# Sliding-window attention into a SwiGLU FFN on one core: constants from a broadcast word, loads ahead of GpSimd's masks, and a new order table

## The chip, the cores and the metric

One core of one Trainium2 chip runs the whole program. The metric is the device time of one execution in microseconds (us). A core has five engines that run their own instruction streams in order: TensorE (PE, matrix products; its weight loads are shown as PEld), VectorE (DVE), ScalarE (ACT), GpSimd (POOL) and SyncE (SP, which here only issues transfers). Streams wait for one another by semaphores. Transfers are issued by an engine and run on 16 DMA engines, which all queues share.

## The reference

Inputs are q, k, v of shape 4 x 8 x 768 x 64 (batch, heads, sequence, head size) and the FFN's weights. Attention is masked to a window of 128 keys and to 4 "sink" keys at the sequence's start; its output becomes x with 3072 tokens x 512.

```python
keep = (pos[None, :] < 4) | ((rel >= 0) & (rel < 128))      # rel = query - key
a = softmax(where(keep, q @ k.T / sqrt(64), -1e9))
x = (a @ v).transpose(0, 2, 1, 3).reshape(3072, 512)
xn = x / sqrt(mean(x * x) + 1e-6) * rms_g
g = xn @ w_gate                                             # 512 x 1536
out = (g * sigmoid(g) * (xn @ w_val)) @ w_out               # 1536 x 512, float32 out
```

## The kernel before

**Blocks and groups.** The 3072 tokens are 24 blocks of 128 (six per batch entry); four blocks make a group of 512 tokens for the FFN, six groups in all. Matrix products take bf16. Lines are those of the kernel before; behind the part that the diff cuts away, a line has a number lower by two in the kernel after.

**Loads.** q and k of block 0 come as float32 through SP's hardware queue and are cast on chip (`load_f32`, L345; the cast, L349). All other blocks of q, k (L353) and v (L357) and all weights (w_gate and w_val L399, w_out in two halves L405) are loads that GpSimd issues on the software queue, casting to bf16 on the way. That queue takes them in order. In the text a load has the name of its tensor and block (q.9, k.6, v.5), or of the weight and its first 128-column part (wg.8). A load of a block from the tenth on needs the scores of ten blocks before, since its buffers are reused. The n-th load also waits until the eighth load before it has landed.

**Transposes.** Scores need q and k with the head dimension on the partitions. Blocks 0 to 7 are transposed on TensorE (`pe_t`, L445) and copied out by DVE or ACT (L452). From block 8 on, SP issues a DMA transpose (`dma_t`, L459). The same split holds for the normalised tokens that feed the FFN: TensorE (L708, copied at L714) for blocks 0 to 7, a DMA transpose by SP (`dma_x`, L720) from block 8 on. SP also issues the stores of the output (L1020). All of SP's transfers stand in one in-order stream: one that waits for its input holds all behind it.

**Attention of a block.** Scores on TensorE (L485, L501, and L563 for blocks cut into triangles), exponentials on ACT (L512, L536, L572), the mask on DVE (L520, L547, L584) for blocks below 16 and on GpSimd as `affine_select` (L526, L597) from block 16 on, then the product with v (L616, L621, and the sink keys' part, L641). In the first two blocks the mask is added by TensorE instead, as a product of the identity with a bias tile (L467). DVE divides (L660, L661), ACT squares (L669), and DVE makes the RMS factor and scales (L676 to L693).

**FFN of a group.** Gate and value products (L975), tanh on ACT (L982), two DVE operations (L988, L998), the output product (`project`, L1008), evacuation on ACT (L1016), the store (L1020). A group's parts are 128 tokens x 4 columns of 128 in group 0, 256 tokens x 2 in groups 1 and 2, and 512 tokens x 1 from group 3 on.

**Constants.** An identity tile and a bias tile are made at the start: DVE sets each to zero (L275, L276), GpSimd's `affine_select` then writes the diagonal (L286) and the triangle (L292). DVE derives the identity without the sink rows (L304), the second bias half (L298) and the masks from them. 56 "warm" products of a zero tile (L421) on TensorE have no effect on the result; they keep that engine running.

**The order.** Every operation is recorded in a `Plan` with what it needs and what it gives. Nothing is scheduled at run time: `ORDER` has, for each engine, the list of operation numbers in the order in which that engine runs them, `TURNS` interleaves the five lists into the order in which the instructions are written out, and `BANKS` names the PSUM bank for each product. `Plan.run` plays the three tables and asserts that each operation's needs have been given before:

```python
        for c in "".join(turns.split()):
            e, ops = ids[c]
            o = self.ops[next(ops)]
            assert o["needs"] <= given, o["gives"]
```

In the kernel before, GpSimd issues the loads up to q.20, then runs the masks of block 16 and of a part of block 17, issues k.20, runs another mask, and so on to v.23. SP's transposes begin q.8, q.9, k.8, k.9, q.10, then the store of block 0, q.11, k.10, k.11.

Of the kernel before, what the change touches and what calls it, by code (L numbers as in the profile page):

```python
# [9 lines left out]
ALU = mybir.AluOpType  # L10
ACT = mybir.ActivationFunctionType
FP32 = mybir.dt.float32
BF16 = mybir.dt.bfloat16
I32 = mybir.dt.int32

P = 128
# [7 lines left out]
NEG = -32768.0  # L24
# [10 lines left out]
class Plan:  # L35
# [5 lines left out]
    def __init__(self):  # L41
        self.ops, self.held = [], {}

    def op(self, ways, needs=(), gives=(), prio=0.0, takes=(), drops=(), ring=None, work=0.0,
           mode=0):
        self.ops.append(dict(
            ways=ways, needs=set(needs), gives=tuple(gives), prio=prio, takes=tuple(takes),
            drops=tuple(drops), ring=ring, work=work, mode=mode, at=len(self.ops),
        ))
# [40 lines left out]
""",  # L90
    "ACT": """
24 20 22 199 177 175 178 176 182 180 181 183 168 188 222 204-206 211 207 212 209 191 210
217 226 228 227 229 195 598 220 236 603 613 618 608 243 633 628 260 623 245 247 246 248
638 278 262 255 264-267 197 280 282 284 653 273 320 648 643 295 297 659 290 322 299 301
300 302 276 324 325 293 326 327 309 664 678 669 683 674 333 312 693 340 316 341 688 342
343 698 355-357 336 358 703 370 371 708 372 318 373 349 385 364 387 718 713 723 739 379
399 401 400 402 728 418 419 733 420 393 421 409 763 758 778 768 754 773 744 749 427 433
414 783 434-436 448 449 793 450 798 451 442 808 788 819 803 463-466 813 457 824 480 475
482 494 496 497 495 513 488 514 515 504 834 838 516 848 843 853 829 863 868 858 878 873
525 883 531-533 893 509 888 534 899 923 549-551 928 552 938 543 567-569 918 570 585 587  # L100
933 943 948 561 953 579 958 909 904 968 593 963 914 973 1008 1003 994 998 1013 1028 1023
989 1038 1018 1033 984 1053 1048 1043 979 1069 1059 1064 1072 1073
""",
    "DVE": """
# [13 lines left out]
""",  # L118
    "POOL": """
25 8 9 26-28 31 34 30 32 37 35 29 38 33 39 41 42 40 43 45 47 44 48 46 49 36 50 53 57 52  # L120
54 51 56 63 62 60 55 58 64 61 59 65-99 467 469 468 470 481 100 483 101-108 517 520 109
518 519 535 538 537 536 110 553 555 554 571 573 556 572 588 586 574
""",
    "SP": """
# [7 lines left out]
ASDDSDGDPDPSPDPPPPPGPPPGPDPGPPDDPGAGPPPPADGPPPPGPPSPDPSADPGSDPSPGAAAPAGPAPPDAPPGPPAPDPAP  # L132
PPPADPGPDAGPPDPPDGAPPGPAPPAGDPAPAPDGADAPDGPAPPPADPAGPDAPADAGPPPPAPADGAPADGPPPPPAPPDPGPPD
DPAGPDPAGPDPGAPDDGPDGPDADGDPDGPADADPGAADPGPGDPADGAPDPGADAPGADADPGDPAPPDAPPDADAPGDPPADAGP
AAGPAPDAPPDPADPDAPGDAPDDGDPAPGDPPGSAAPGADAPGDPDGPPPDAGDAPGDADPPGADPAGDSAPPAGASPADPADSADP
PPGADAPGPSADDPGASAPGDPGSAPPGDPSADGAPDASDAPPDADPAGPPSAAADPAADPADPDAPAGADPGADPPDAPPADDPDGS
PDAPASAGDPPAPAGDSPADAPADDPPAGSADPPDASDPAGPADPSDDPGAPDDPADAPDGSDPDGPAGAPADSAPPADSDPPDGPDS
PDAGASPAAPDASGDPADSPDSDPGSPPPDDPSDGPDADPAPADPSDPSPDPSPDDAPDPDAPADPADAPDADAPDPDPASAPDASAP
DSADPADPDPASAPASADPAPPDASDPDAPSDASPADPDADPDPDPDAPASAPPDASADPAGPDGPGDPDGAPDPDPDPDAPAAGPSA
# [16 lines left out]
def kernel(  # L156
# [128 lines left out]
    def make_ident():  # L285
        nc.gpsimd.affine_select(  # L286
            out=ident, in_=ident, compare_op=ALU.not_equal, fill=1.0,
            base=0, pattern=[[-1, P]], channel_multiplier=1,
        )
# [851 lines left out]
```

## Time and profile before

| | us |
|---|---|
| median of 3 runs (lowest, highest) | 241.71 (241.26, 241.87) |
| the profiled execution, its own time | 243.59 |
| its span | 241.9 |
| TensorE busy in it | 231.3 (96%) |
| DVE busy | 187.4 (77%) |
| ACT busy | 122.8 (51%) |
| GpSimd busy | 89.2 (37%) |
| granted TensorE clock, mean | 1.000 of full speed |

The profile is one execution, recorded by the hardware. Its page has the busy time of each engine (part 1), the span in 40 equal slices of about 6 us with the busy share in tenths (part 2), the DMA queues (part 3), the chain of work that ended last (part 4), and the costliest groups of instructions (part 5). Further views are the waits (engine, line, what it waited for: total, times, longest), the chain as a list in order of time, a timeline, and a table of stretches: for each stretch its length, then the busy time of PE, PEld, DVE, ACT and POOL (with the number of instructions), the granted clock, the mean DMA share and GB/s. In a stretch an instruction counts where it starts. A DMA's time is from its issue to its landing.

### The profile page before, as it was taken

What the parts mean: (1) busy time and instruction counts of PE and PEld (TensorE: products, weight loads), DVE (VectorE), ACT (ScalarE), POOL (GpSimd) and SP (SyncE); (2) the same over time, 40 slices, a digit from 0 to 9 for tenths busy, and PEclk for the clock granted to TensorE, in tenths of its full rate; (3) what the DMA queues carried; (4) which work ended last, traced back from release to release, by engine and by line L of the source; (5) the groups of instructions that cost most, each with busy time, mean ns of one, the idle gap of its engine ahead of it and who ended that gap; (6) DMA issues with size and microseconds to landing.
All of it is one profiled execution on the core that took longest, in us unless ns stands there. A gap on an engine that the chain in (4) does not pass through costs nothing.

```text
span 241.9 us, 5897 instructions
## 1 busy us (share of the span) xinstructions
PE 231.3 (96%) x2329; PEld 147.6 (61%) x2354; DVE 187.4 (77%) x478; ACT 122.8 (51%) x267; POOL 89.2 (37%) x116
## 2 busy tenths in 40 slices
PE   7889999999879999999999999999999999999995
PEld 5568986876668776777876644445554444444443
DVE  3599989989979999999898989994569946537520
ACT  4776368667766574337654464454543321233112
POOL 8985894597526554000004982022540000000000
PEclk9999999999999999999999999999999999999999
DMA  9999999999999999999601999527010114101024
GB/s 128 143 183 195 182 178 194 162 143 139 137 151 152 138 143 154 132 233 156 126 2 24 119 150 123 131 70 128 3 23 0 32 36 173 43 0 47 0 87 173
DMA packets 113741, 27.42 MB, mean 113 GB/s; under 512 B 103857, under 2 KB 110769, under 8 KB 113714
## 3 DMA queue, kind: packets, MB, share of 16 engines
q0 software_dynamic: 81760, 13.90, 79.3%
q1 hardware_dynamic: 31810, 12.95, 29.8%
q8 instruction: 18, 0.29, 0.5%
q10 hardware_dynamic: 144, 0.20, 0.2%
q14 instruction: 9, 0.07, 0.1%
HBM read 28.35 MB, written 6.29 MB: 143 GB/s over the span
## 4 chain that ended last, share of the span: by engine, by line
PE 67%; DMA 20%; POOL 6%; issue 2%; DVE 2%; SPq 2%; POOLq 0%
PE v L975 20%; PE o L1008 20%; PE g L975 18%; DMA wo<-in_moe_w_out_dram 5%; DMA qkT<-q 4%; DMA wv<-in_moe_w_val_dram 4%; DMA wg<-in_moe_w_gate_dram 3%; DMA q<-in_q_dram 3%; POOL v L357 2%; SPq L459 2%; PE s L563 2%; PE av L621 2%; POOL k L353 1%; PE av L616 1%; PE o_last L1028 1%
## 5 line engine op out<-in xcount | busy, mean ns | idle before, releaser
L975 PE MATMUL v<-xnt,wv 128*128 128x128 bf16 (+2 forms) x527 | 72.2, 282 | 0.4 <-DMA wv<-in_moe_w_val_dram 0.2
L975 PE MATMUL g<-xnt,wg 128*128 128x128 bf16 (+2 forms) x521 | 71.3, 281 | 0.4
L1008 PE MATMUL o<-wo,hT 128*128 128x512 bf16 x259 | 65.3, 379 | 1.1 <-issue 0.5
L982 ACT ACTIVATE th<-g 128x512 bf16<-128x512 f32 x72 | 41.7, 599 | 48.4 <-PE g L975 48.2
L988 DVE SCALAR_TENSOR_TENSOR p<-th,g 128x512 bf16<-128x512 bf16 x72 | 48.1, 682 | 18.9 <-ACT th L982 18.7
L975 PEld LDWEIGHTS <-wv 128*128 128x128 bf16 x528 | 43.3, 98 | 21.3 <-DMA wv<-in_moe_w_val_dram 0.6
L998 DVE TENSOR_TENSOR hT<-p,v 128x512 bf16<-128x512 bf16 x72 | 48.1, 682 | 9.3 <-PE v L975 7.8
L975 PEld LDWEIGHTS <-wg 128*128 128x128 bf16 x528 | 42.8, 98 | 19.3 <-issue 1.0
L1008 PEld LDWEIGHTS <-hT 128*128 128x128 bf16 x276 | 25.4, 98 | 26.5 <-issue 0.2
L597 POOL TENSOR_SCALAR_AFFINE_SELECT e<-e 128x512 bf16<-128x512 bf16 x20 | 12.7, 656 | 54.4 <-ACT e L572 53.0
L572 ACT ACTIVATE e<-s 128x384 bf16<-128x384 f32 x52 | 23.1, 495 | 12.5 <-PE s L563 12.5
L1016 ACT ACTIVATE osb<-o 128x512 f32<-128x512 f32 x23 | 13.4, 597 | 21.8 <-PE o L1008 18.0
L357 POOL DMA_DIRECT2D v<-in_v_dram x24 | 21.3, 888 | 8.5 <-DMA q<-in_q_dram 3.8
L353 POOL DMA_DIRECT2D q<-in_q_dram x23 | 20.4, 891 | 9.9 <-DMA k<-in_k_dram 6.7
L353 POOL DMA_DIRECT2D k<-in_k_dram x23 | 20.4, 889 | 9.1 <-DMA v<-in_v_dram 4.5
L669 ACT ACTIVATE sq<-x 128x512 bf16<-128x512 bf16 x24 | 15.1, 631 | 14.8 <-DVE x L661 14.5
L661 DVE TENSOR_TENSOR x<-av,rden 128x256 bf16<-128x256 f32 x48 | 20.4, 424 | 1.7
L693 DVE SCALAR_TENSOR_TENSOR xr<-x,r,gb 128x512 bf16<-128x512 bf16 x24 | 18.7, 778 | 0.8
L621 PE MATMUL av<-v,e 128*128 128x65 bf16 x192 | 16.4, 193 | 0.3 <-DMA v<-in_v_dram 0.3
L536 ACT ACTIVATE e<-s 128x512 bf16<-128x512 f32 (+1 forms) x36 | 15.1, 519 | 1.6 <-PE s L485 1.5
L616 PE MATMUL av<-v,e 128*128 128x65 bf16 x160 | 14.8, 193 | 0.0
L621 PEld LDWEIGHTS <-e 128*128 128x128 bf16 x192 | 12.7, 97 | 2.8 <-DVE e L547 0.4
(78 smaller groups left out, 192.6 us busy)
## 6 DMA issues: line engine op xcount, KB each, us to landing
out_dram<-osb SPq DMA_DIRECT2D x23, 256.0 KB, 2.2
v<-in_v_dram POOLq DMA_DIRECT2D x24, 128.0 KB, 8.9
q<-in_q_dram POOLq DMA_DIRECT2D x23, 128.0 KB, 8.1
k<-in_k_dram POOLq DMA_DIRECT2D x23, 128.0 KB, 9.6
wo<-in_moe_w_out_dram POOLq DMA_DIRECT2D x2, 768.0 KB, 11.3
wg<-in_moe_w_gate_dram POOLq DMA_DIRECT2D x5, 256.0 KB, 8.0
wv<-in_moe_w_val_dram POOLq DMA_DIRECT2D x5, 256.0 KB, 8.9
stage<-in_k_dram SPq DMA_DIRECT2D x1, 256.0 KB, 3.0
```

The source lines that it names most:

```text
L353: nc.gpsimd.dma_start(out=T[name, g], in_=block_of(src, g))
L357: nc.gpsimd.dma_start(out=V16[b][:, t, :, 0:D], in_=block_of(v, g))
L572: nc.scalar.activation(out=e_tile(g)[:, x:x + 2, 0:TW], in_=BANK.pop(("s", g, u, hi))[:, 0:2 * TW].rearrange("p (j c) -> p j c", c=TW), fu ...
L616: nc.tensor.matmul(out=dest, lhsT=T["e", g - 1][:, x, P:2 * P], rhs=V16[b][:, t - 1, h, :], start=(t == 1), stop=False, skip_group_check=True,
L621: nc.tensor.matmul(out=dest, lhsT=T["e", g][:, x, 0:P], rhs=V16[b][:, t, h, :], start=(t == 0), stop=True, skip_group_check=True,)
L661: nc.vector.tensor_tensor(out=T["x16", g][:, 4 * u:4 * u + 4, :], in0=pvv[:, :, 0:D], in1=rden.unsqueeze(2).to_broadcast((P, 4, D)), op=AL ...
L693: nc.vector.scalar_tensor_tensor(out=T["xr", g], in0=T.pop(("x16", g)).rearrange("p h d -> p (h d)"), scalar=r[:, 3:4], in1=gb, op0=ALU.mu ...
L975: nc.tensor.matmul(out=ps[:, i * n:(i + 1) * n], lhsT=w_sb[:, kt, ft * P:(ft + 1) * P], rhs=T["xnt", G][:, kt, cols], start=(kt == 0), sto ...
L982: nc.scalar.activation(out=T["th", key], in_=BANK[("g", key)], func=ACT.Tanh, scale=0.5,)
L988: nc.vector.scalar_tensor_tensor(out=T["p1", key], in0=T.pop(("th", key)), scalar=1.0, in1=BANK.pop(("g", key)), op0=ALU.add, op1=ALU.mult,)
L998: nc.vector.tensor_tensor(out=T[hk][:, i:i + n, cols], in0=T.pop(("p1", key)).rearrange("p (n c) -> p n c", n=n), in1=BANK.pop(("v", key)) ...
L1008: nc.tensor.matmul(out=BANK[("o", G, tb)], lhsT=T["h", G, ft // 4][:, ft % 4, tb * P:(tb + 1) * P], rhs=wo[:, ft, :], start=(ft == 0), sto ...
```

## The change

Two memsets by DVE go, and with them two operations of the plan, so all numbers shift by two (1077 operations become 1075). The two `affine_select`s read a constant of the program, a float32 zero broadcast over 128 x 128, in place of the tile that they write; they need nothing any more. `Plan` gets a table of aliases that is empty. `ORDER`, `TURNS` and `BANKS` are new; `...` marks what is cut.

```diff
-        self.ops, self.held = [], {}
+        self.ops, self.held, self.alias = [], {}, {}
...
-            ways=ways, needs=set(needs), gives=tuple(gives), prio=prio, takes=tuple(takes),
+            ways=ways, needs={x for t in needs for x in self.alias.get(t, (t,))}, gives=tuple(gives), prio=prio, takes=tuple(takes),
...
     "POOL": """
-25 8 9 26-28 31 34 30 32 37 35 29 38 33 39 41 42 40 43 45 47 44 48 46 49 36 50 53 57 52
-54 51 56 63 62 60 55 58 64 61 59 65-99 467 469 468 470 481 100 483 101-108 517 520 109
-518 519 535 538 537 536 110 553 555 554 571 573 556 572 588 586 574
+6 7 23 24 41 25 29 32 28 30 47 26 35 31 27 39 37 36 40 38 33 45 43 44 42 46 51 48 34 50
+52 55 61 49 53 62 58 57 54 59 56 60 63-108 465 467 466 468 481 479 518 515 517 516 533
+535 534 536 551-553 569 571 570 554 584 586 572
...
-    dve(70, lambda: nc.vector.memset(ident, 0.0), gives=["id0"], prio=-99)
-    dve(230, lambda: nc.vector.memset(bias.bitcast(I32), 0), gives=["bias0"], prio=-98)
...
-            out=ident, in_=ident, compare_op=ALU.not_equal, fill=1.0,
+            out=ident, in_=nc.const_aps.tensor(0.0, (P, P), FP32), compare_op=ALU.not_equal, fill=1.0,
...
-            out=bias[:, 0, :], in_=bias[:, 0, :], compare_op=ALU.is_ge,
-            fill=NEG, base=0, pattern=[[1, P]], channel_multiplier=-1,
+            out=bias[:, 0, :], in_=nc.const_aps.tensor(0.0, (P, P), FP32),
+            compare_op=ALU.is_ge, fill=NEG, base=0, pattern=[[1, P]], channel_multiplier=-1,
...
-    pool(270, make_ident, ["id0"], ["ident"], -89.2 + POOL_AT[0])
-    pool(270, make_bias, ["bias0"], [("bias", 0)], -89.1 + POOL_AT[1])
+    pool(270, make_ident, (), ["ident"], -89.2 + POOL_AT[0])
+    pool(270, make_bias, (), [("bias", 0)], -89.1 + POOL_AT[1])
```

In names, the new lists differ in this:

- GpSimd: identity and bias first, then q.1, k.1, wg.8, v.0, q.2, q.3, v.1, k.2, q.4, wg.0 and the other weights in a new order. Then q.5, k.4, v.3, the first half of w_out, k.5, q.6, q.7, v.4, v.5, k.7, q.8, v.6, the second half of w_out, k.8, k.6, v.8, v.7, q.9, k.9 and so on to v.23: all loads, and only then the masks of blocks 16 and later. Before, the part from q.7 ran: second half of w_out, q.7, v.8, q.8, v.5, k.6, k.7, k.8, v.6, v.7, q.9, k.9.
- SP: transposes and stores run q.8, store of block 0, k.8, q.9, k.9, q.10, store of block 2, k.10, q.11, q.12, k.11, k.12, q.13, xr.8 and so on; later q.17, q.15, q.16, xr.11, xr.10, k.15 follow the store of block 1.
- TensorE: the same operations but for the order. Two warm products stand ahead of the first bias product (15 before) and nine behind it; about 20 stand singly among the first FFN products, the last of them near the place that has the 62nd microsecond before, five of them behind the transpose of k.6.
- DVE and ACT: the cast of q of block 0 and the copies of the transposed q.1 and q.5 move from ACT to DVE; the copies of the transposed k.0, xr.2 and xr.3 move from DVE to ACT.

More of the change, by code (lines that the diff above doesn't have):

```diff
@@ L71 @@
     "PE": """
[18 rows of a table removed]
[18 rows of a table added]
 """,
     "ACT": """
[L92 to L102, printed above, removed]
+22 18 170 175 173 176 180 178 174 166 179 186 181 220 204 202 205 203 209 189 207 208
@@ new lines @@
+210 215 226 224 227 225 193 218 596 234 601 611 258 237 616 241 631 245 246 606 626 243
+244 621 636 260 253 262-264 278 265 195 256 280 646 282 651 318 271 641 293 288 295 657
+320 297 299 298 300 662 322-325 274 291 307 676 667 310 681 331 314 338 339 691 340 686
+672 341 696 353-356 334 701 368 347 369 370 711 706 716 316 371 721 383 385 737 362 399
+397 377 400 726 398 416 391 417 731 418 419 761 766 756 752 747 776 771 781 407 431 432
+742 433 412 434 425 791 446-448 796 786 817 806 449 440 461-463 801 464 811 455 822 478
@@ L103 @@
+480 473 492 494 495 493 827 511 486 512 841 836 846 513 502 514 861 832 856 851 523 876
+871 866 886 529 530 881 891 531 507 532 547-549 897 926 550 565 566 907 921 567 541 941
+568 916 936 583 585 951 559 577 902 931 956 912 966 946 591 971 961 992 996 982 1001 977
+1006 1011 1021 1026 1016 1036 1041 1031 1051 1046 987 1067 1057 1062 1070 1071
 """,
     "DVE": """
[13 rows of a table removed]
[13 rows of a table added]
 """,
     "POOL": """
-25 8 9 26-28 31 34 30 32 37 35 29 38 33 39 41 42 40 43 45 47 44 48 46 49 36 50 53 57 52
-54 51 56 63 62 60 55 58 64 61 59 65-99 467 469 468 470 481 100 483 101-108 517 520 109
@@ L131 @@
 TURNS = """
[L132 to L137, printed above, removed]
@@ L138 @@
-PDAGASPAAPDASGDPADSPDSDPGSPPPDDPSDGPDADPAPADPSDPSPDPSPDDAPDPDAPADPADAPDADAPDPDPASAPDASAP
-DSADPADPDPASAPASADPAPPDASDPDAPSDASPADPDADPDPDPDAPASAPPDASADPAGPDGPGDPDGAPDPDPDPDAPAAGPSA
-DGPAASGPADSPAGDPPGDDPGPPDGPDAAGPPDAGADPAGPAAGDPADAGPGPDSPGDPDASGPDGAADSPDAPDSDPPDSPDAPDS
-ADPDSAPPDSDPSDAPDASPADDPDPDPADAPAAPDASADPADSPGSDGPDGSPGPGPAPAPADPAPDADPADAPDAGAPDGPGPAAP
-AAPPADGDPPDGPDGDGPPAAPDSPGDPGAGPDAPPDPDPDPDAADPADPDDPAPAADPSDPDPDDPAAPPSPDDPAAPDPPSPPDPA
-PSDSDSPASDPDPPPAAPDDPDPDPPAAPSDPDPAPDDPDPPPPAAPDADPSDPAAPDPDPAAPDDPDPDAPADPDPDPDPPDPAAPD
@@ L144 @@
-SPSDPPPPPAAPSASSPAADS
+ASDGDGSDPGPDSDDPGDGPPPAPGPPPPPPGPPDAGPPSDGDSPDSPPGSPPPAPADGADAAPGAPPPADPGADPGAPPPAGPDAPG
+PAPGAPPDAPDAGPAPADPGPAPDAGDPADPAPPPAGPDAGPAPPPPADAPGADPAPPDDGPPDGAPDPAGPPPPGPPPDPDAPAGPP
+DAGPDDPAPGADPGDPGPAPDPAGAPGADAPPDGADPAPGDDPAGDDPDPPPPADPPPDAGDAPDPGADAPGPPAAGPAPDPAPDPGP
+AAPGDDPGAPDAGSDPADDGPDPPPDADAPPDAPGDPADGPDAGDPPAGPPADGAPSADSGAPASPAPDGAPDSPDAAPPDAPPGPDA
+PADGSAPPDAGPDGPDAPPAGPSPGSDPPDASDAPDAPDPADPAGAPAADPAADPPGSADPDAPSAADPPGSAPDPADGAPDDPDPDA
+PGSAADGPADPAGPPADSGAPPDPDSAPDAADSPDGPPDDGDPAPDAPDAPADAPDGDPDDPAAPGADPSAGPPADADSPSDPGDDSP
@@ new lines @@
+GPDAADPAAPGADPADPDDPPGSPPDGDPSDGPPPSGDPSPAGADPSADAPDASDPDGSPDSPDDGPADAPGDADAPGDPDDPGPAAP
+ADASPGADSAPADSPAGPDASAPPADGSPDPADSDPAPASDPADAPDSADPDPDPASDAPASAPPADASGPDPGDSPGDSGPADAPDP
+PDDPDPAAPASGPDAGADPAPADPAPDPPDASDPPPADDAPADPAPADSAPDADPASDGPGSPDPSDGSPDAGAPSDDPAPPDSASDP
+DPSDDAPSDAPDAPDSASDPDPDADPDPDPDPAAPASADPADAPADPGDGDPGPGPAAPPADPADPAAPDGPGPAGAPAAPSADAPDP
+DAPAPGAPDGPADGPDGDPPDDPPAAGPPDSPGDPDGAPADPDPPDPDAPDAPAPDDPAPDPAPASPSDADPDAPPDSPDPSDSDPDP
+AAPDSPDPDDPDPPPAPPPPAAPPAAPDSDPPAPDPADPDPDDPDPAPDPAAPDPDPDDPAPDPADPDAPADPDPDDPDPAAPDSDPS
@@ L145 @@
+DSPPPPAPAPSASSPAADS
 """
 BANKS = """
-0123456701234567012345645645635654353513714370432704614654154761061305147237235720165760
-7615743764051726351402376152376015237653746573746574631547613547647136210735462047136524
-7012473650241762350741602735410721356421305406354063420675134632745013274350174362507431
-6542371607152374153275461237104573604156324175032407615342047562310462317460170414217326
-5047314243270172316412040572153042573045
+0123456701670167016017601760426041732757373224736750120120732073256403716537653143725163
@@ L152 @@
+0454730721563047635704163157610250174065061760157460516743050176431503256043125603571420
+3652740136257417546035243761057456130721305723057012657310625710476512476041736250413625
+7430612572532610752356731205374567214076531420731647021537025631725460253047210452317236
+5734165062705273462065430654350724064521
 """
```

70 rows, old and new, of the table ORDER are left out of this document.

## The prediction

> **What bounds the kernel.** I read the page's busy shares and slices first, then the table of stretches, then the waits, and last the chain between 47 and 76 us. TensorE carries the kernel:
>
> ```profile
> PE 231.3 (96%) x2329; PEld 147.6 (61%) x2354; DVE 187.4 (77%) x478; ACT 122.8 (51%) x267; POOL 89.2 (37%) x116
> ...
> PE   7889999999879999999999999999999999999995
> ...
> PEclk9999999999999999999999999999999999999999
> DMA  9999999999999999999601999527010114101024
> ...
> q0 software_dynamic: 81760, 13.90, 79.3%
> q1 hardware_dynamic: 31810, 12.95, 29.8%
> ```
>
> Only three places have room: the first slices, slices 11 and 12 (60 to 72 us), and the last. The DMA row is full up to 114 us: there the software queue (all loads that GpSimd issues) and the hardware queue (SP's) share the engines. The stretches say how much is open (PE's busy time is the third number):
>
> ```profile
> 6.00:12.00 6.00, 5.39 (x62) 3.16 (x61) 3.44 (x14) 4.26 (x13) 6.00 (x9) 1.00 1.85 142
> ...
> 60.00:66.00 6.00, 5.22 (x74) 3.77 (x72) 5.61 (x21) 3.98 (x9) 3.27 (x5) 1.00 2.33 126
> 66.00:72.00 6.00, 4.68 (x81) 3.75 (x70) 4.66 (x8) 4.22 (x10) 2.26 (x3) 1.00 1.60 151
> 72.00:78.00 6.00, 6.00 (x106) 4.95 (x104) 5.32 (x12) 3.45 (x9) 3.05 (x4) 1.00 1.98 150
> ```
>
> From 72 to 234 us each stretch of 6 us has 5.84 or more: nothing is to be won there, only lost. The waits give what stands in the gap, and the chain (start, length, what) gives its history:
>
> ```profile
> PE s L563 <- DMA qkT<-q: 1.3, 1, 1.3
> ...
> PE s L563 <- DMA qkT<-k: 0.8, 1, 0.8
> ```
>
> ```profile
> 47.27 7.30 DMA q<-in_q_dram
> 54.59 1.20 SPq L459
> ...
> 59.75 10.61 DMA qkT<-q
> 70.35 0.14 issue
> 70.49 0.54 PE s L563 x16
> ```
>
> q.9 is loaded until 54.57 us. SP's queue, which runs in order, stands at its transpose until then, though k.8, next in line, had landed at 51.34. The transpose of q.10 is issued at 59.75 and lands at 70.34, and the scores of block 9 start at 70.49. By PE's own timeline the scores of block 8 waited 0.95 us (64.7 to 65.7) and those of block 9 1.49 (69.0 to 70.5): 2.44 us in all.
>
> **The change, part by part.**
>
> *Constants.* DVE loses two memsets (0.11 and 0.17 us, at 0.89 and 1.24). GpSimd's two selects (0.30 and 0.29, at 2.42 and 2.66) now come ahead of q.1's issue (1.32 to 2.32). So identity and bias are ready about 1.1 us sooner and q.1's issue goes out about 0.6 later; k.1 and all behind it keep their place. Whether a select that reads a broadcast word in float32 costs more than 0.30, no row shows; twice that would be 0.6 on GpSimd, on q.1 alone. TensorE's first use, the mask bias at 3.30, can start earlier, but the first transpose (4.72) waits for block 0's k (landed 3.83) and its cast (0.62 on ACT), which do not change. Gain on the path 0; if that cover went, up to 1.1.
>
> *Warm matmuls.* Before, 15 of the 56 run ahead of the mask bias; after, 2 do, 9 run behind it, and about 20 stand singly among FFN work up to the 62nd microsecond. One costs 0.055 us at full clock. Those ahead of the transpose of k.6 fill waits for loads; five stand behind it: 5 x 0.055 = 0.28 us, hidden if TensorE waits for transposes there anyway, else paid.
>
> *Head, loads up to 31 us.* One half-width weight part (128 columns, 0.4 to 0.7 us by the landings of such parts) and q.4 (0.9) move ahead, and others back. The last weight goes about one load later; TensorE's order was moved to match. Bounds -0.3 and +0.5, since the stretches 12 to 18 and 18 to 24 us leave PE 1.04 and 0.08 us open in all, and the loads still land one after another; I take +0.1.
>
> *The loads of k.6.* Counted from the two orders, k.7, v.6 and k.8 now stand ahead of k.6 in the software queue and v.8 behind it: two loads more. The queue lands one q, k or v load per 0.9 us (45.92, 46.99, 47.80, 48.86, 49.59, 50.49), so k.6 goes from 49.59 to about 51.4. The transpose of k.6 began at 50.32 and was itself waiting for that load. The useful work ahead of it is the same in both orders (37.8 us), so it starts 1.1 to 2.2 us later, depending on how much the transpose of q.8, issued about 2 us sooner, takes from the loads. I take 1.6. The second half of w_out goes five loads back (44.98 to about 49.5) and binds the same stretch, no later than that.
>
> *SP's order.* Now q.8, the first store, k.8, q.9, k.9, q.10. The transpose of k.8 no longer waits for q.9's load, but the store waits for a projection and its evacuation (near 53 us). SP issues a transpose per 1.2 to 1.3 us, at times 2.5. So q.10 is issued at 58 to 59.5, against 59.75. The work ahead of the scores of block 9 is 55.1 us in both orders, that ahead of block 10's 59.9. If the transposes land by about 69.8, the 2.44 us of waits go, and the 1.6 us that k.6 came late eat most: late work at k.6 simply shortens the wait at block 8. For block 10 a store now stands ahead of k.10's transpose and q.11's behind it: issue near 64 against 64.92, just in time for scores that start at 75.4 less the gain.
>
> A transpose takes 6.9 to 10.6 us from issue to landing while loads are queued, and 2.4 with none (at 113.36 and 114.70). Between these two rows lies what the whole change turns on:
>
> ```profile
> q0 software_dynamic: 22692, 2.87, 193.3%
> ...
> qkT<-q SPq DMA_TRANSPOSE x5, 7.7
> qkT<-k SPq DMA_TRANSPOSE x4, 9.6
> ```
>
> (44 to 72 us; the packet times of one queue alone add up to almost twice the engines' time, that is, packets lie there waiting.) I take the upper row, as 40 to 100 us are like that stretch.
>
> The Trainium skill ("DMA: Bandwidth & Descriptors", section "Queues, rings and completion order") says that each DMA engine goes round-robin between its queues, a packet at a time. By that alone a transpose would get every other turn and take about twice its lone 2.4 us, an estimate of 5; the trace has 6.9 to 10.6 and does not agree, unless the packets of the two queues differ much in length. By the rule, the loads that now stand ahead of the masks could not crowd the transposes, and the slow rival below would be worth nothing.
>
> *Loads ahead of masks.* Before, v.20 and ten more loads were issued behind the masks of blocks 16 and later, from 133 us on, and the queue ran dry at 110.50. After, all are issued ahead. Each needs scores of ten blocks before, done by then, and eleven at 0.9 us or a little more keep the queue full to about 120. What hides it: nothing needs those blocks before 133. What it can cost: transposes issued between 104 and 112, which took 2.4 to 7.5, may take 8 to 10. The scores of block 15 and the FFN part fed by the transposes of blocks 10 and 11 (near 115 us) then come 0 to 1.5 late; I take 0.3. Masks sit behind issues of 0.87 us each, but GpSimd stood idle from 96 to 126, so they are not late.
>
> *Sum.* -2.44 + 1.6 + 0.1 + 0.1 (a third of the warm matmuls) + 0.3 = -0.34; with the small waits of projections for v.5 and of q.4's transpose (0.48 and 0.54 us, before) half gone, since q.4 moved up, -0.6. Against the profiled execution's 243.59 that is 243.0; its span is 241.9, and the median of the runs, 241.71, is what the forecast stands on: 241.1. A difference of 0.3% (0.73 us) is about what a measurement of this kernel can tell from no change.
>
> **Rivals.**
>
> 1. *Transposes land as before.* The queue is as full as before and the loads in it come no sooner, so what is issued at 58.5 lands at 70 all the same; k.6's delay then lies inside the same wait. Scores of blocks 9 and 10 start as before: 241.7. For it: the landing of q.10's transpose came after a 10.6 us pass. Against it: k.8 lay ready for 4.5 us behind another load.
> 2. *Both stalls vanish and k.6 costs less.* k.6 late by 1.1 and nothing lost near 115: -2.44 + 1.1 + 0.1 = -1.24, or 240.5. For it: the loads ahead are counted, and 0.9 x 2 less the slack of 0.7 between the landing of k.6 and its start is 1.1.
> 3. *The crowded queue, slower.* The transposes of blocks 10 to 17 meet a software queue that no longer runs dry at 110.5. Its place: the scores of block 15 and the FFN part behind xr.11. Its price: a landing of 8 to 10 us where 2.4 to 7.5 was seen, less the lead of 4 to 6 us which TensorE's order leaves, is 1 to 3 us; it decides once transposes issued at 104 to 107 land after about 115. With the other terms: +0.4 to +2.4, centred on 243.0. Against it: before 100 us, transposes of 8.6 us cost TensorE nothing, as the full stretches from 72 on show.
> 4. *The clock rises later.* Warm matmuls were spaced 0.105 us up to the 5th microsecond and 0.055 behind it: TensorE starts at half speed. With fewer of them at the start the step could come later by 1 to 3 us, on work that fills 75% of the time there, so 0.5 to 1.5; but that work waits for loads (k.1 landed at 7.42), which hides most: 242.0.
>
> The Trainium skill ("TensorE: Matmul & The Clock Gate", section "What's actually happening") asks for about 3.4 us of sustained busy time before full clock; the trace's step near 5 us, with TensorE busy from 1.33, agrees. By that rule thinner work at the start is what would delay the step, as rival 4 has it.
>
> **How the numbers follow.** Forecast, between -0.2 and -1.0: 0.36; rival 1: 0.16; rival 2: 0.14; rival 3: 0.27; rival 4: 0.07. Faster by over 0.3% is rival 2 and half of the forecast, with a little of the forecast's upper half: 0.34. Slower is rival 3 and a part of rival 4: 0.30. The rest, 0.36, lies within. The range leaves out a tenth at each end: below, past rival 2's 240.5 by the 0.9 us that the head may still hold, 239.6; above, the upper end of rival 3, 243.9. The forecast's own range is 240.7 to 241.5.
>
> **What would show it.** Right: the chain no longer has a transpose of about 10 us before the scores of block 9; PE's busy time in 60 to 72 us rises from 9.9 to 11 or more, while 48 to 54 falls below 5.5, by the wait for k.6, with its transpose starting near 51.9. Wrong: scores of block 9 still wait for a transpose past 70.5 (rival 1); a new wait of scores or of the FFN for a transpose between 110 and 120 (rival 3); a stretch from 6 to 12 us below 5 (rival 4); a wait for weights between 15 and 31 us that was not there.

## The result and the profile after

The kernel after takes 244.53 us (median of 4 runs, 243.98 to 244.74), the kernel before 241.79 in the same series: a ratio of 1.0101, with a 95% interval of 1.0070 to 1.0132. It is slower by 2.7 us, where 0.6 less was forecast; the range ended at 243.9.

The page of the kernel after (busy times, slices, the software queue):

```profile
PE 232.5 (96%) x2329; PEld 148.1 (61%) x2354; DVE 188.4 (78%) x476; ACT 122.1 (50%) x267; POOL 90.9 (38%) x116
...
PE   6998999989999999999999999999999999999995
...
PEclk9799999999999999999999999999999999999999
...
q0 software_dynamic: 81760, 13.90, 84.5%
```

Its stretches (length, busy time of PE, PEld, DVE, ACT, POOL, granted clock, DMA share, GB/s):

```profile
6.00:12.00 6.00, 5.44 (x49) 3.06 (x50) 2.78 (x11) 3.33 (x11) 6.00 (x8) 0.78 2.28 155
...
18.00:24.00 6.00, 4.89 (x85) 4.26 (x82) 4.74 (x15) 3.97 (x10) 3.62 (x6) 1.00 1.48 195
...
48.00:54.00 6.00, 5.21 (x60) 3.23 (x59) 5.68 (x19) 3.93 (x10) 3.48 (x4) 1.00 2.43 149
...
60.00:66.00 6.00, 5.53 (x55) 3.96 (x55) 5.64 (x19) 2.89 (x6) 3.50 (x5) 1.00 2.42 144
66.00:72.00 6.00, 6.00 (x98) 4.63 (x97) 5.77 (x15) 5.25 (x13) 2.43 (x3) 1.00 1.75 161
```

Most of what the forecast wanted to see is there. TensorE's busy time from 60 to 72 us rises from 9.90 to 11.53, scores wait for no transpose there, and 48 to 54 falls from 5.52 to 5.21, where the transpose of k.6 starts at 51.93 (51.9 was forecast). And yet this profiled execution took 243.98 us against 243.59 for the profiled one of before. So the first question is what that profile of before stood for: it lay 1.9 us above its own median.

### The profile page after: what moved, and what is told of

It is laid out like the page before. It is cut to its first block, busy times and chain, and to the rows that moved or that the text cites. A ratio compares the mean times of both kernels' runs of the same rounds, so it can differ in the third digit from the quotient of the medians.

```text
span 242.3 us, 5896 instructions
## 1 busy us (share of the span) xinstructions
PE 232.5 (96%) x2329; PEld 148.1 (61%) x2354; DVE 188.4 (78%) x476; ACT 122.1 (50%) x267; POOL 90.9 (38%) x116
## 4 chain that ended last, share of the span: by engine, by line
PE 73%; DVE 20%; issue 2%; DMA 2%; ACT 1%; SPq 0%
PE o L1006 21%; PE v L973 20%; PE g L973 19%; DVE p L986 4%; DVE x L659 3%; DVE hT L996 3%; DVE r L687 3%; DVE e L582 2%; PE s L561 2%; PE av L619 2%; DVE xr L691 2%; DMA stage<-in_q_dram 2%; PE av L614 1%; PE s L483 1%; PE o_last L1026 1%
## 5 line engine op out<-in xcount | busy, mean ns | idle before, releaser
L973 PE MATMUL v<-xnt,wv 128*128 128x128 bf16 (+2 forms) x523 | 70.5, 281 | 0.2
L980 ACT ACTIVATE th<-g 128x512 bf16<-128x512 f32 x72 | 41.2, 598 | 50.4 <-PE g L973 50.0
L986 DVE SCALAR_TENSOR_TENSOR p<-th,g 128x512 bf16<-128x512 bf16 x72 | 47.6, 680 | 18.8 <-ACT th L980 18.8
L996 DVE TENSOR_TENSOR hT<-p,v 128x512 bf16<-128x512 bf16 x72 | 47.7, 683 | 6.2 <-PE v L973 4.9
L595 POOL TENSOR_SCALAR_AFFINE_SELECT e<-e 128x512 bf16<-128x512 bf16 x20 | 13.3, 686 | 49.0 <-ACT e L570 48.7
L691 DVE SCALAR_TENSOR_TENSOR xr<-x,r,gb 128x512 bf16<-128x512 bf16 x24 | 19.2, 801 | 0.8
L534 ACT ACTIVATE e<-s 128x512 bf16<-128x512 f32 (+1 forms) x36 | 15.8, 522 | 4.9 <-PE s L483 4.9
```

The source lines that it names most:

```text
L691: nc.vector.scalar_tensor_tensor(out=T["xr", g], in0=T.pop(("x16", g)).rearrange("p h d -> p (h d)"), scalar=r[:, 3:4], in1=gb, op0=ALU.mu ...
L973: nc.tensor.matmul(out=ps[:, i * n:(i + 1) * n], lhsT=w_sb[:, kt, ft * P:(ft + 1) * P], rhs=T["xnt", G][:, kt, cols], start=(kt == 0), sto ...
L980: nc.scalar.activation(out=T["th", key], in_=BANK[("g", key)], func=ACT.Tanh, scale=0.5,)
L986: nc.vector.scalar_tensor_tensor(out=T["p1", key], in0=T.pop(("th", key)), scalar=1.0, in1=BANK.pop(("g", key)), op0=ALU.add, op1=ALU.mult,)
L996: nc.vector.tensor_tensor(out=T[hk][:, i:i + n, cols], in0=T.pop(("p1", key)).rearrange("p (n c) -> p n c", n=n), in1=BANK.pop(("v", key)) ...
```

## The experiments

Two kinds of number are used below. Times are medians, with ratios to the kernel before on the same chip. "TensorE's lag" at a point of time is that time less the work done by then, with each operation priced at what its kind takes in the trace of before when nothing is in its way (lower quartile of the distances from start to start), and warm products priced at nothing. It shows where time was lost, and whether it was made up. A wait is the idle time that the timeline shows ahead of an instruction.

| us of lag at | 14 | 29 | 47 | 62 | 77 | 230 |
|---|---|---|---|---|---|---|
| before, first profile (243.59) | 8.42 | 11.04 | 12.20 | 12.96 | 15.61 | 18.58 |
| before, second profile (241.90) | 8.13 | 10.92 | 11.71 | 12.53 | 13.95 | 16.91 |
| after, first profile (243.98) | 8.29 | 12.44 | 13.26 | 14.89 | 15.85 | 18.99 |
| after, second profile (244.93) | 8.29 | 12.71 | 13.53 | 15.82 | 16.78 | 19.93 |
| after, middle loads as before (242.44) | 8.29 | 12.24 | 13.07 | 13.81 | 14.31 | 17.44 |
| before, k.8 ahead of q.9 (241.56) | 8.43 | 11.49 | 12.59 | 13.17 | 13.64 | 16.56 |
| before up to 48, then after (242.45) | 8.29 | 11.48 | 12.31 | 13.69 | 14.28 | 17.42 |
| before, both edits that won (240.98) | 8.05 | 11.11 | 11.82 | 12.56 | 13.07 | 15.94 |

**1. The kernel before, profiled again.** No edit.

> The kernel before, unchanged. Its profiled execution (243.59 us) stood 1.8 us above the median of its runs, while the profiled execution of the kernel after (243.98) stood 0.5 below its own. Theory 1: the wait of the scores of blocks 8 and 9 for transposes (2.44 us in that profile) is part of every execution; a new profile near 241.7 shows it again, and the 1.8 us lie elsewhere. Theory 2: the wait came with that execution only; a new profile near 241.7 has less than 0.7 us of it, so the change had nothing to win there.

241.9 us in the profiled execution, 242.05 median. Its waits and stretches:

```profile
PEld L563 <- DMA qkT<-k: 1.2, 1, 1.2
...
PE s L563 <- DMA qkT<-k: 0.9, 1, 0.9
```

```profile
60.00:66.00 6.00, 5.08 (x75) 3.57 (x73) 5.62 (x19) 4.09 (x9) 3.57 (x5) 1.00 2.48 129
66.00:72.00 6.00, 6.00 (x94) 5.12 (x91) 5.27 (x9) 4.50 (x11) 1.75 (x2) 1.00 1.72 160
```

Half of either theory holds. The wait of block 8 for k.8's transpose (0.92 us ahead of the scores at 65.38, 0.78 in the first profile) is there again. The wait of block 9 for q.10's (`PE s L563 <- DMA qkT<-q` in the first profile) is gone: TensorE is busy through 66 to 72, where the first profile had 4.68. That wait is 1.32 us by the timeline and 1.49 by the forecast's count, which begins 0.17 us earlier, within the product ahead. So 1.5 of the 2.44 us that the change was to win belonged to one execution and not to the median; no other execution of before on record takes more than 242.98 us.

**2 to 4. Head, head and middle, tail.** The first hybrid runs after's orders up to 31 us and then before's, the second after's up to 75 us, the third before's up to 75 us and then after's.

```diff
 ORDER[engine]
-[all operations in the order of before]
+[operations of after that start before 31 us (75 us)] + [the rest in the order of before]
 (the third: operations of before that start before 75 us, then the rest in the order of after)
```

> The kernel after's constants and its orders up to 31 us on every engine, and from there the orders of before. Theory H (the head costs: warm matmuls thinned out, the clock lower from 6 to 18 us, q.4 and another weight part ahead): slower than before by 2 us or more, 243.8 or above. Theory M (loads of k.6 and what follows): within 0.7 us of before, 241.1 to 242.5.

> The orders of after up to 75 us on every engine, then those of before. Theory H: as the first hybrid, 243.8 or above. Theory M (k.6 late by 1.6 us with nothing won at blocks 8 and 9): 243 to 244, while the first hybrid is near before. Theory L (the late part, loads ahead of masks crowding transposes): within 0.7 us of before.

> The orders of before up to 75 us, constants as before, then the orders of after, with all loads ahead of the masks. Theory L: slower than before by 2 us or more, 243.8 or above. Theories H and M: within 0.7 us of before, 241.1 to 242.5.

243.75 (1.0071, 1.0053 to 1.0088), 244.76 (1.0113, 1.0093 to 1.0133) and 242.05 (1.0000, 0.9987 to 1.0013). The whole loss lies before 75 us. Loads ahead of GpSimd's masks cost nothing that the interval (0.3 us to either side) can tell: in the third hybrid loads land until 125.27 us, the transposes issued between 102 and 121 whose landing is known take 6.7 to 8.7 us, and TensorE stays busy:

```profile
102.00:108.00 6.00, 6.00 (x58) 5.38 (x56) 5.58 (x13) 3.38 (x8) 4.29 (x5) 1.00 2.15 151
108.00:114.00 6.00, 5.90 (x63) 3.83 (x63) 5.68 (x14) 4.28 (x11) 1.85 (x3) 1.00 1.77 162
114.00:120.00 6.00, 6.00 (x87) 4.79 (x85) 5.47 (x15) 3.18 (x7) 0.00 (x0) 1.00 1.93 177
120.00:126.00 6.00, 5.95 (x77) 4.49 (x76) 5.75 (x15) 4.56 (x11) 0.58 (x1) 1.00 1.65 120
```

The first hybrid can't be read as the cost of the head: its lag grows by 1.6 us between 32 and 35 us, at the seam, where loads and products come from different plans. It is no proof for theory H.

**5. The counterpart, before's head with after's rest**, cut at 31 us too.

```diff
 ORDER[engine]
+[operations of before that start before 31 us] + [the rest in the order of after]
```

> The orders of before up to 31 us, then those of after; constants by the broadcast word. If the parts add up (head 1.5, middle 1.0, late 0): 243.0. If all of the loss is in the head: within 0.7 us of before's 242.0. If the head's delay hides what the middle would cost alone: above 243.5.

245.29 (1.0139, 1.0117 to 1.0160). It has the same fault: 3.5 us of its lag arise between 32 and 38 us, at the seam, where the profiled execution also has the granted clock at 0.50 from 35.02 to 38.43. The one execution of the four with a mean clock of 1.000 takes no less, 245.30. The run is inconclusive.

**6. The middle loads alone.** The kernel after with before's order from the first half of w_out to v.7.

```diff
 POOL: ... v.3
-wo.0 k.5 q.6 q.7 v.4 v.5 k.7 q.8 v.6 wo.6 k.8 k.6 v.8 v.7
+q.6 wo.0 k.5 v.4 wo.6 q.7 v.8 q.8 v.5 k.6 k.7 k.8 v.6 v.7
 q.9 k.9 ...
```

> The kernel after with GpSimd's loads from the first half of w_out to v.7 in the order of before (k.6 three places earlier, the second half of w_out five). Theory K (k.6 late: its transpose starts at 51.9 to 52.9 instead of 49.9, with a wait of 0.7 to 1.3 us ahead of it): 0.7 to 1.3 us less than after, 243.2 to 243.8. Rival (what k.6 loses is taken from the wait at the scores of block 8): no change, 244.3 to 244.8, with a wait of 1 us back at blocks 8 or 9.

242.44 (1.0034, 1.0012 to 1.0056; executions from 242.27 to 244.82): 2.1 us less than after by the medians, 1.6 to 2.0 by the ratios, more than theory K named. k.6 lands at 48.73 in place of 51.9 to 52.9. The stretches:

```profile
48.00:54.00 6.00, 5.95 (x67) 3.75 (x65) 5.65 (x19) 4.84 (x12) 5.37 (x7) 1.00 2.62 143
54.00:60.00 6.00, 5.89 (x86) 4.27 (x86) 5.82 (x14) 4.99 (x12) 5.27 (x6) 1.00 2.26 170
60.00:66.00 6.00, 5.95 (x82) 4.18 (x82) 5.61 (x21) 3.58 (x9) 1.75 (x2) 1.00 1.81 144
```

Not only 48 to 54 is full again, but also 60 to 66, where after had 5.53. Nothing is taken back at block 8 or 9. So the late k.6 seems to have a second price, which is read from the trace and not tested alone: the late scores of blocks 6 and 7 make DVE late, which has 5.0 to 5.8 us of work in each 6 from 48 to 72 us in after, and TensorE then waits for it (0.41 us ahead of the transpose of xr.6 at 64.41 in after's first profile).

**7 and 8. Which of the late loads.** k.6 and k.7 exchanged, and the second half of w_out moved forward.

```diff
 POOL (7): ... v.5
-k.7 q.8 v.6 wo.6 k.8 k.6 v.8
+k.6 q.8 v.6 wo.6 k.8 k.7 v.8
 POOL (8): ... q.7 v.4
-v.5 k.7 q.8 v.6 wo.6 k.8 k.6 v.8
+wo.6 v.5 k.7 q.8 v.6 k.8 k.6 v.8
```

> The kernel after with k.6 and k.7 exchanged in GpSimd's list, nothing else: k.6 lands near 43.5, k.7 near 52. Theory K6 (the late k.6 is what costs): its transpose no longer waits, 0.7 to 1.3 us less than after's 244.5, so 243.2 to 243.8. Rival W2 (the second half of w_out, landing near 49 to 51 instead of 44, is the load that holds TensorE, through the projections that need it): no change, 244.2 to 244.8, and the wait moves to a projection or to the transpose of k.7.

> The kernel after with the second half of w_out moved to behind v.4 in GpSimd's list (it lands near 45 instead of 49 to 50); k.6 keeps its place near 52. Theory K6: no change, 244.2 to 244.8, the transpose of k.6 still starts at 52 to 53. Theory W2: 0.7 us or more less, 243.8 or below.

243.41 (1.0053, 1.0036 to 1.0070) and 242.87 (1.0043, 1.0025 to 1.0060): 1.1 and 1.7 us less than after by the medians. The intervals of runs 6, 7 and 8 overlap, so which of them wins most is not settled. Neither theory is alone right, and the second run is not as clean as its expectation held, because k.6 landed sooner there as well, at 51.03. The landings show why. In after the loads end at v.6 44.71, w_out 49.21, k.8 51.05, k.6 51.89; in the second profile of before at v.4 41.10, w_out 44.48, and k.6, k.7, k.8 at 49.08, 50.04, 50.89. The same half of w_out takes 4.5 us in place of 3.4, and with the two loads behind it 7.18 in place of 5.38 (to v.8 at 46.48). Between them runs the transpose of q.8 (SP's timeline, first after, then the second profile of before):

```profile
43.74 1.31 SPq L457 DMA_TRANSPOSE qkT<-q  x1
...
47.36 1.31 SPq L459 DMA_TRANSPOSE qkT<-q  x1
```

In after it lands at 50.71, and its 0.13 MB move between 47.7 and 49.8 us, while w_out and k.8 are on their way. In before they move between 50.6 and 53.6, when k.8 (50.89) has all but landed. After's order issues it 3.6 us sooner, and so about 1.8 us seem to be taken from the loads that TensorE waits for; no run moves this transpose alone. With w_out forward, q.8 lands at 48.19 and its transpose meets loads behind k.8.

**9. The exchange on SP.** The kernel before with one exchange.

```diff
 SP: ... qT.8
-qT.9 kT.8
+kT.8 qT.9
 kT.9 qT.10 st.0.0 ...
```

> The kernel before with one exchange in SP's list: the transpose of k.8 ahead of that of q.9, which waits for a load. Theory S (in before, the scores of block 8 wait about 1 us for k.8's transpose, which stands behind the one of q.9): k.8's transpose is issued near 51 instead of 55.7, the wait goes, 0.7 to 1.1 us less than before's 241.9: 240.8 to 241.2. Rival (the transposes move through a full queue and land no earlier, or the wait moves to block 9): within 0.4 us of before.

241.16 (0.9974, 0.9959 to 0.9989): 0.78 us less than before, and theory S holds. SP's timeline in this run (start, length, instruction; lines are five higher than in before), and TensorE's:

```profile
48.06 1.30 SPq L464 DMA_TRANSPOSE qkT<-q  x1
51.51 1.19 SPq L464 DMA_TRANSPOSE qkT<-k  x1
54.74 1.19 SPq L464 DMA_TRANSPOSE qkT<-q  x1
```

```profile
64.07 1.04 PE L980 MATMUL g<-xnt,wg 128*128 128x256 bf16 x8
65.03 0.54 PE L568 MATMUL s<-qkT 64*64 64x192 bf16 x24
```

The transpose of k.8 is issued at 51.51, right behind its load, in place of 55.69, and lands at 59.78 in place of 65.34. The scores (L568) follow the product ahead of them without a wait. Issued 4.2 us sooner, it landed 5.6 us sooner.

**10. The hole on TensorE near 18 us.** In after, TensorE waits 0.85 us ahead of the transpose of xr.1 at 19.63. Before had u.0.0.0 and the transpose of k.3 there. The first attempt moved u.0.0.0 and two loads, the second was made on top of run 6.

```diff
 PE (both):    ... g.0.0.0 +u.0.0.0 ... (taken from behind g.0.4.128)
 POOL (first): ... k.2 -q.4 wg.0 wg.2 v.2 wv.0 +q.4 +wg.8 ...   (wg.8 taken from behind k.1)
 POOL (second): ... v.2 wv.0 +wv.2 wg.6 wg.4 +q.4 wv.6 wv.4 +wg.8 k.3 ...
```

> The kernel after, with q.4 and wg.8 behind wv.0 in GpSimd's list (two loads fewer ahead of wv.0) and the value product u.0.0.0 directly behind its gate product, as before. Theory H (a hole on TensorE near 18 to 20 us, which u.0.0.0, 0.89 us, filled before): 0.7 to 1.0 us less than after's 244.5, so 243.5 to 243.8, and the lag of TensorE at 29 us that much smaller. Rival W (the cost of the head is the warm matmuls that stand among work): no change, 244.3 to 244.8.

> As the run with the middle loads in the order of before (242.4), and at the head wv.2 directly behind wv.0, q.4 and wg.8 behind wg.4 and wv.4, and u.0.0.0, which needs wv.0 and wv.2, directly behind g.0.0.0. Theory H (TensorE's hole of 1 us near 18.5 us, filled by u.0.0.0 before): 0.6 to 0.9 us less than the run without this edit, 241.5 to 241.8, and TensorE's lag at 29 us smaller by as much. If the head costs nothing that lasts: 242.2 to 242.6.

The first took 248.5 us (1.0261): u.0.0.0 needs wv.2 as well as wv.0, and that lands at 22.97, so TensorE stood 4.9 us. The edit left this out, and the run tells nothing of theory H. In the second u.0.0.0 starts at 17.60 and waits 0.70 us for wv.2 in its middle (landed at 18.88), so the hole is filled in part; the run took 242.46 us (1.0025, 1.0011 to 1.0040), as without the edit (242.44). Its lag at 20 us is about 0.5 smaller than in run 6, but at 29 us it is 12.34 against 12.24: TensorE waits 0.27 and 0.30 us for the next tokens (at 20.98 and 25.97) instead. Filling that hole so far wins nothing.

**11. Without the late warm products.** The 27 that stand behind g.0.0.0 are left out.

```diff
     def warm(i):
+        if i in LATE:
+            return
```

> The kernel after without the 27 warm matmuls that stand behind the first gate product (they have no effect on the output). Theory W: 27 x 0.055 = 1.5 us at most, of which those in waits cost nothing; about 20 stand in stretches with no wait: 1.1 us less, 243.4. Theory H: 0 to 0.4 less, 244.1 to 244.5. If the clock needs them, slower than after and a granted clock below 1.0 behind 20 us.

245.25 (1.0121, 1.0085 to 1.0158; executions from 243.65 to 246.08), against 244.53 to 245.03 for after. The 1.1 us less of theory W are not there, though with this scatter a few tenths can't be excluded. In the profiled execution TensorE waits 1.57 us for w_out, a wait that after's profiles do not have, and 1.15 for k.6 (0.73 and 1.25 in after).

**12. All of them early.** Run 6 with those 27 in the first 6 us.

```diff
 PE: warm x2 +warm x13 mb.0 warm x9 kp.0 warm x2 +warm x14 qp.0 ...
```

> The run with the middle loads in the order of before (242.4), and the 27 late warm matmuls moved to the first 6 us, 13 of them ahead of the first mask bias. Theory HW (of the head's 1.2 us, 0.5 to 1 are warm matmuls in the way and a lower clock near 10 us): 241.5 to 241.9. Rival HL: no change, 242.2 to 242.7, whatever the clock does.

244.87 (1.0117, 1.0090 to 1.0145), 2.4 us more than run 6. It was more than a test of the clock: 13 warm products at half rate move the mask bias from 2.02 to 3.34 and k's first transpose from 4.64 to 6.01, and 14 more move q's from 5.40 to 9.00. What it shows is another thing: the head is on the path. Its lag at 29 us is 14.57 against 12.24, and 2.0 of these 2.3 us are still there at the end of the profiled execution (244.45 against 242.44).

**13. The constants alone.** The kernel before with the new constants, and the selects ahead of q.1.

```diff
-    dve(70, lambda: nc.vector.memset(ident, 0.0), gives=["id0"], prio=-99)
-    dve(230, lambda: nc.vector.memset(bias.bitcast(I32), 0), gives=["bias0"], prio=-98)
...
+            out=ident, in_=nc.const_aps.tensor(0.0, (P, P), FP32), compare_op=ALU.not_equal, fill=1.0,
...
 POOL: -q.1 ident bias k.1
 POOL: +ident bias q.1 k.1
```

> The kernel before with the change to the constants alone: no zeroing by DVE, the two selects read the broadcast word and stand ahead of q.1's issue. All other orders as before. Theory as in the prediction: no effect on the path, within 0.3 us of before's 241.9. Rival (q.1's issue 0.3 to 0.6 us later delays the whole software queue and the head with it): 0.4 to 0.8 us slower, 242.3 to 242.7.

241.55 (0.9981, 0.9970 to 0.9993): 0.4 us less, where both theories had nothing or a loss. The mask bias starts at 2.83 in place of 3.31, k's first transpose at 4.55 in place of 4.87. Which of it lasts is not settled: at 62 us TensorE is no further than in the second profile of before. In its profile the gain is at block 8, whose wait is 0.53 in place of 0.92 us. The software queue fits that: k.1 is issued at 2.57 in place of 2.91, q.9 lands at 53.83 in place of 54.38, and k.8's transpose behind it at 64.83 in place of 65.34.

**14. Two loads early.** The kernel before with wg.8 and q.4 where after has them.

```diff
 POOL: q.1 ident bias k.1 +wg.8 v.0 wg.0 q.2 q.3 v.1 k.2 +q.4 wg.2 k.3 wv.0 ...
```

> The kernel before with the loads of wg.8 and q.4 at the places that after gives them (behind k.1 and behind k.2), all else as before. Theory HL (the head of after costs about 1.2 us because these two loads, 1.3 to 1.6 us of the queue, stand ahead of the weights that TensorE needs from 16 to 26 us): 0.9 to 1.5 us slower than before, 242.8 to 243.4. Rival: what is late there is made up by 31 us, when the last weight lands as before: within 0.5 us of before.

243.0 (1.0050, 1.0026 to 1.0073; executions from 241.94 to 244.57): 1.0 us slower. In before's order these two loads cost what theory HL says, but a part of it may be the clock: in the profiled execution (244.42) it stands at 0.50 from 22.39 to 25.80 us, and the four executions with a mean clock of 0.999 or more take 241.94 to 243.16. That the same holds in after isn't shown: there TensorE's order was changed with them, and run 10 moved them back without a gain.

**15. The kernel after, profiled again.** No edit.

> The kernel after, unchanged, for a second profile, as its first one lay 0.5 us under the median. Expected near 244.6, with k.6 landing near 53 instead of 51.9 and a wait of over 1 us ahead of its transpose; if instead the head holds the difference, TensorE's lag at 29 us is 0.4 or more above that of the first profile.

245.03 median (1.0116, 1.0092 to 1.0140), the profiled execution 244.93. The chain from 41 us on (start, length, what):

```profile
41.41 11.46 DMA k<-in_k_dram
52.87 0.05 issue
52.92 0.40 PE k L443 x4
```

The first guess holds: k.6 lands at 52.87, with a wait of 1.25 us ahead of its transpose. The lag at 29 us is 0.27 above that of the first profile, less than the 0.4 of the second guess.

**16. before's first 48 us, then after with the middle loads of before.** Cut where both plans expect nearly the same loads and products.

```diff
 ORDER[engine]
+[operations of before that start before 48 us] + [the rest in the order of run 6]
```

> The orders of before up to 48 us (constants too), then those of after, with GpSimd's middle loads in the order of before, so that both halves expect the same loads. Theory HO (the other 1.2 us of the loss lie in after's first 48 us, in the order of its operations as a whole, and after's SP order wins its 0.75): 241.0 to 241.5. Rival: they lie behind 48 us, the stores ahead of transposes or the loads ahead of masks: 242.2 to 242.7, as the run with the middle loads alone.

242.44 (1.0029, 1.0018 to 1.0039), as run 6. By 47 us it is 0.76 ahead of run 6, and by 62 us 0.12: 0.41 us go in a wait at the seam (the product with v at 48.94) and 0.26 ahead of k.6's transpose. It settles neither theory.

**17. Both edits that won, on the kernel before.** The constants of run 13 and the exchange of run 9.

```diff
 POOL: -q.1 ident bias k.1
 POOL: +ident bias q.1 k.1
 SP:   -qT.8 qT.9 kT.8
 SP:   +qT.8 kT.8 qT.9
```

> The kernel before with two edits: the constants of after (and their selects ahead of q.1's issue), and the transpose of k.8 ahead of that of q.9 in SP's list. If the two gains add (0.41 and 0.78 us): 240.8. If both shorten the same wait at the scores of block 8: no better than the exchange alone, 241.1 to 241.3.

240.93 us (0.9957, 0.9944 to 0.9970): faster than both kernels, by 1.0 us than before and 3.6 to 4.1 than after. Whether the gains add is not settled. 240.93 lies between 240.8, expected if they do, and 241.1 to 241.3, expected if both shorten the wait of block 8, and the interval overlaps that of run 9 (0.9959 to 0.9989). The profile of run 13, where that wait is the shorter by 0.39 us, speaks for the second.

```profile
60.00:66.00 6.00, 6.00 (x83) 4.40 (x82) 5.65 (x19) 4.76 (x11) 4.68 (x6) 1.00 1.83 162
66.00:72.00 6.00, 6.00 (x93) 5.18 (x91) 5.93 (x12) 4.31 (x10) 2.24 (x3) 1.00 1.74 150
```

## Why the prediction was wrong

The two profiles that lie near their medians, 241.90 and 244.93, differ by 3.03 us. By the lag they part like this: +1.79 up to 29 us, +0.03 from there to 47, +1.47 to 62, -0.46 to 77 and +0.19 to 230, 3.02 in all.

- **SP's order, -2.44.** This step failed first. 1.49 of the 2.44 us, the wait of block 9, was in the profiled execution only, which lay 1.9 us above its median. The forecast took the gain from that execution and set it against the median, and the text had both numbers side by side. Without this term the forecast's own sum is +1.8 us, 243.6. The mechanism is right in part: run 9 shows that one exchange of it wins 0.78 us on the kernel before. In after the waits for transposes are gone too, but nothing shows that SP's order won that: the scores of block 8 start at 66.70 and 67.63 us there, behind 65.34, where k.8's transpose lands in the second profile of before, so TensorE's lateness alone would have hidden the wait. And q.10's transpose, forecast to be issued at 58 to 59.5, is issued at 59.96, no sooner than in before (59.75 and 59.50).
- **The loads of k.6, +1.6.** The mechanism was right, and so was the start of the transpose in the first profile (51.9 forecast, 51.93 measured); that it fits to 0.03 is luck, since the second profile has 52.92. The term was sized too small: giving the old order back wins 2.1 us by the medians. The bounds had 2.2 with q.8's transpose in the way, and the traces fit that: w_out and the two loads behind it took 1.8 us longer with it among them. One reading was wrong: in the first profile of before the transpose of k.6 did not wait for its load, which had landed 0.73 us ahead of it; rival 2 had that slack. The second part of the price, that DVE gets late behind k.6, was not named.
- **"Late work at k.6 simply shortens the wait at block 8."** Right as far as that wait goes, 0.9 us in the second profile of before; the lag shows 0.46 of it taken back between 62 and 77 us. Past that, nothing was left to absorb it.
- **The head, +0.1.** This failed too. The lag at 29 us is 12.24 to 12.83 in the runs with after's head (those that change nothing ahead of it) and 10.92 to 11.58 in those with before's. "TensorE's order was moved to match" was an assumption; it is not what the rows say. The place is known, its cause isn't settled: the late warm products (run 11) and the hole near 18 us (run 10) do not account for it. Two early loads cost 1.0 us in before's order (run 14), but moving them back in after wins nothing. The casts and copies that changed places between DVE and ACT were not tested alone, and the attempts to give after the other head lost the difference at a seam (runs 5 and 16).
- **Constants, 0.** They win 0.4 us (run 13). The select that reads the broadcast word isn't slower (0.29 us against 0.30). That k.1 and all behind it keep their place was wrong: k.1's issue comes 0.34 us sooner. That k's transpose is bound by its load and cast alone was wrong by 0.3 us: it also came behind the mask bias on TensorE.
- **Warm products, +0.1, and loads ahead of masks, +0.3.** Leaving out the late warm products wins nothing that shows in the scatter, and the late loads cost nothing (1.0000). The place of rival 3, the one that ended clearly slower, was thus wrong, and that its sign was right is luck; no rival joined a late k.6 with a slow head.
- **Rivals 1 and 2** went by block 9's wait as well: with it gone from the ordinary execution, neither "as before" nor the gain of 1.24 us could come out.
- **The sum.** Half of 0.48 and 0.54 is 0.51, which takes -0.34 to -0.85 and not to -0.6, and the upper end of rival 3 is 241.71 + 2.4, or 244.1, not 243.9. Neither slip changes the sign, and 244.53 lies above both.
- **Rival 4, the clock.** The granted clock did fall, which is told below, but at no cost that shows: the lag at 14 us is 8.29 in after, where it fell, and 8.29 in run 6, where it did not. Of the eight executions of after, four have a mean clock of 0.991 to 0.993 and take 243.79 to 245.13 us; the other four, at 0.999 or more, take 244.34 to 245.21.

The rule of the Trainium skill ("DMA: Bandwidth & Descriptors", section "Queues, rings and completion order"), by which each DMA engine goes round-robin between its queues, agrees with the trace in one half: the loads did slow down while a transpose ran (4.5 us for 3.4). It does not fit the time of a transpose as a whole: k.8's took 8.27 us in run 9, and 2.4 us is what one took where no load was queued. But q.8's moved its data within 2.1 us in after (47.7 to 49.8); it is the 4.0 us ahead of that and the 0.9 behind it that the rule does not account for.

## What to carry to other kernels

Look at how a profiled execution stands to the median before pricing a wait that it shows; a wait which comes once can't be won, and a second profile costs little. When a load is moved, follow what its earlier landing sets off: here q.8, loaded sooner, released a transpose whose packets met the very loads that TensorE needed next. In an in-order queue, an entry whose input is there should not stand behind one whose input isn't: one exchange of that kind won 0.3%.

## What the runs showed of the hardware that had not been expected

- **Loads and transposes slow each other, and by how much depends on what is queued.** A transpose lands 7 to 10 us behind its issue among loads and 2.4 us without. With q.8's transpose among them, half of w_out and the two loads behind it took 7.18 us in place of 5.38. Of that transpose's 7 us the first 3 to 4 passed before its data moved (issued at 43.74 in after, moving from 47.7; at 47.36 in before, moving from 50.6).
- **The granted clock fell to half in the head of after**, for one stretch of 3.4 us, and the busy share ahead of it does not tell why. The rows are, in this order, two of after's first profile, one of run 6, and two of run 5 (the columns are those of the stretches above):

```profile
6.00:9.39 3.39, 2.83 (x33) 1.72 (x33) 1.62 (x6) 1.28 (x5) 3.39 (x5) 1.00 2.19 155
9.39:12.80 3.41, 3.41 (x25) 1.95 (x26) 1.86 (x9) 2.28 (x8) 3.41 (x6) 0.50 2.22 157
...
4.80:8.21 3.41, 2.70 (x39) 1.75 (x36) 1.51 (x4) 1.16 (x4) 3.41 (x5) 1.00 1.93 141
...
32.00:35.02 3.02, 0.89 (x14) 0.64 (x14) 0.56 (x1) 2.26 (x5) 1.80 (x3) 1.00 1.90 181
35.02:38.43 3.41, 3.41 (x36) 3.41 (x34) 3.31 (x7) 0.88 (x2) 2.56 (x3) 0.50 1.60 190
```

  In after TensorE was busy for 2.83 of the 3.4 us ahead of the fall. In run 6 it was busy for 2.70 in the stretch from 4.80, and the clock stayed at 1.00. In run 5 it was busy for 0.89 of 3.0 us ahead of a fall. The Trainium skill ("TensorE: Matmul & The Clock Gate", section "What's actually happening") gives half speed after an idle window of about 3.4 us; run 5 is near that, but in after a stretch that was 83% busy came ahead of it, and no stretch was idle for that long. The runs do not show where the bound lies. Run 6 has after's order throughout its head, so the order alone does not decide it.
- **Two executions of one program differed by 1.7 us, 1.3 of them in one wait for a transpose** (the two profiles of before), with the same granted clock of 1.00.
